# Stacked weight tails, two more separate tiles, and moved weight splits in the last stages of a transformer block

## The chip, the core and the metric

The kernel runs on one core of a Trainium2 chip. The metric is the device time of one execution in microseconds (us). The kernel before has a median of 2336.36 us over three runs (2336.26 to 2337.21). One further execution was profiled; its own time is 2338.7 us. A measurement of this kernel can tell about 0.2% from no change.

## The reference

A pre-norm transformer block on 2048 tokens of width D = 576, all in float32. The attention has 32 query heads of 18 values, with one key head and one value head that all share. The feed-forward part (FFN) is a bilinear gate without a nonlinearity and has hidden width F = 4608.

```python
h  = x + softmax((LN(x) @ wq)_heads @ (LN(x) @ wk).T / sqrt(18)) @ (LN(x) @ wv) @ wo
g, u = LN(h) @ w_gate, LN(h) @ w_up
h2 = h + (g * u) @ w_down
```

## The kernel before

**Tiles.** The tokens are cut into four blocks of 512 (block 0 to 3), the hidden width into 36 tiles of 128 (`NF`), taken in 18 pairs (`NC`). Products that need float32 accuracy are made of three passes: an operand is cast to a rounded float32 (the high part, line 88), the rest is its low part (a subtraction on VectorE, line 89), and high*high, high*low and low*high are added up on TensorE. `split` makes both parts; the engine of its cast can be given.

**The order of the work** is written out by hand: the program issues each engine's instructions in the order in which the Python code runs, and each engine works through its own list in that order, waiting where an operand is not ready. All DMAs are issued by SyncE (SP), also in order; SP also waits there until the buffer that a load writes is free.

**Stages.** (1) Layer norm, keys, values, queries and the attention of block 0. In it `sums` (line 1402) prepares on GpSimd the weights of the last stages: `t_dram` holds the tails of the gate and up weights (rows 512 to 575 of the 576, as high and low parts, two halves of 32 rows each, and their four sums), `s_dram` the sums of the other rows for the joint tiles. (2) `ffn(0)`, `ffn(1)` and `ffn(2)` go through the hidden tiles of one block each, with the attention of the later blocks put between their matmuls while pairs of it are left (`more`). `ffn(2)` stops at tile `F1` = 28; the attention ends in its tile 23, so its tiles 24 to 27 run without it. There each tile is 54 half-height matmuls of 512 columns into `gu` (line 992), and after every second tile one down product. Beside them run the last output projections of the attention for block 3 (`project`, line 754), its layer norm statistics and, by `prepare` and `transposed` (line 1057), the normalised and transposed operands of block 3 (`xh`, `bt`, `btt`). The weights of a tile are loaded to `wr` and split by `split_w`, its cast on GpSimd; GpSimd also casts `wos`, the output weights, in `split_wo`. (3) `two_blocks` (line 1240). Its first loop, here called the **separate stage**, makes tiles 0 to 27 of block 3. A tile is four products (`product`, line 1206): two into bank `jx` for the gate, two into `jy` for up. A product is seven matmuls: six on the two 128-row chunks of one weight operand, and a last one on its 96 tail rows (high, high and low part, 32 rows each). After every odd tile follows the down product of an earlier pair. The second loop, here the **joint stage**, makes tiles 28 to 35 of blocks 2 and 3 together: four weight parts against four data parts in seven products rather than eight, then again one down product per tile, for the pairs of block 2 and 3 in turn. (4) The down products of the last pair, and the output.

**The down product** (`down`, line 893) has 14 stages of three matmuls over three PSUM banks (`STAGES`). Eight stages are added to `h` by VectorE (line 954), six are copied by ScalarE (line 958) and added by GpSimd (line 959). A stage that reuses a bank waits until the bank was read.

**What feeds a product.** `ahead(tails, splits)` (line 1192) keeps two counts. Up to `tails` products it loads the tails from `t_dram` to a slot of `ws_j` (in the joint stage also of `X`), with three DMAs of 32 rows (line 1197). Up to `splits` products it casts the raw operand (ScalarE, line 88), subtracts (VectorE, line 89) and starts the load of the raw operand eight further on (line 1190). A slot is used again six products on, in the joint stage eight. `refill(n)` calls it after every product with n + 6 tails and n + 4 splits, in the joint stage n + 8 and n + 5. After a down product `finish` loads seven weight tiles `wdo` for a later one (`load_wd`, line 865). `left_parts` (line 1218) makes the left operands of the next down product in four steps, here called the left parts, and `differences` (line 1098) makes the data parts of the joint stage in some 28 steps, both as generators that the tile loop advances.

Of the kernel before, what the change touches and what calls it, by code (L numbers as in the profile page):

```python
# [25 lines left out]
P = 128  # L26
# [28 lines left out]
class Block:  # L55
# [652 lines left out]
    def split_wo(self):  # L708

        if self.wo_r and not self.wos and self.wo_round + 1 < self.round:  # L710
            c = min(self.wo_r)
            w = self.wos[c] = self.wp.tile([P, 2, D], F32R, tag="wos", bufs=1, name=f"wos{self.round}_{c}")
            self.split(w[:, 0], w[:, 1], self.wo_r.pop(c), self.nc.gpsimd.tensor_copy)
            if c == 3:
                self.load_wo(4)
# [131 lines left out]
    def load_w(self, n):  # L847

        if n < N_OLD:
            r = self.wr[n] = self.wp.tile([P, 9, P], F32, tag="wr", bufs=1, name=f"wr{n}")  # L850
            self.sp.dma_start(r, self.wgu[n % NF])

    def split_w(self, n):
        if n < N_OLD:
            r = self.wr.pop(n)
            w = self.ws[n] = self.wp.tile([P, 2, 9, P], F32R, tag="ws", bufs=2, name=f"ws{n}")
            self.split(w[:, 0], w[:, 1], r, self.nc.gpsimd.tensor_copy)
            self.load_w(n + 1)
# [333 lines left out]
    def ahead(self, tails, splits):  # L1192

        while self.n_tail < min(tails, len(SEQ)):
            f, o = SEQ[self.n_tail]
            for k in range(3):
                self.sp.dma_start(f32(self.slot(self.n_tail)[32 * k:32 * k + 32, 4]),  # L1197
                                  self.t_dram[f // 9, 32 * (k // 2):32 * (k // 2) + 32, f % 9, o])
            self.n_tail += 1
        while self.n_split < min(splits, len(SEQ)):  # L1200
            w = self.slot(self.n_split)
            self.split(w[:, 0:2], w[:, 2:4], self.raws[self.n_split % 8])
            self.load_raw_operand(self.n_split + 8)
            self.n_split += 1
# [7 lines left out]

    def refill(self, n):

        joint = n > 4 * F1
        self.ahead(n + (8 if joint else 6), n + (5 if joint else 4))

# [22 lines left out]
    def two_blocks(self, pair):  # L1240
# [10 lines left out]

        def finish(head, rest=lambda: None):
            if not head:
                rest()
                return
            b, p, parts = head
            drain(parts)
            for i, _ in enumerate(self.down(b, p)):
                if i == 3:
                    rest()  # L1260
            if not (b == 2 and p >= F1 // 2):
                self.load_wd(self.n_wd + 7)

        hid = []
        for f in range(F1):
# [3 lines left out]
            for i, (bank, B) in enumerate(((x, 0), (x, 1), (y, 0), (y, 1))):  # L1269
                self.product(bank, n, self.B[B], i % 2 == 0)  # L1270
                n += 1
                if i == 1:
                    g = self.hh.tile([P, TB], F32, tag="g", bufs=1, name=f"g3_{f}")
                    act.copy(g, x)
                self.refill(n)
                if not odd:
                    next(head[2], None)
                else:
                    next(work, None)
# [3 lines left out]
            if odd:  # L1283
                finish(head, hidden)
                queue.append((3, f // 2, self.left_parts(False, hid, A)))
                hid = []
            else:
                hidden()
                drain(head[2])
        drain(work)  # L1290
# [7 lines left out]
        for f in range(F1, NF):  # L1298
# [3 lines left out]
            for i, (bank, B, first) in enumerate(plan):  # L1302
# [12 lines left out]
                elif i == 5:  # L1315
                    add(u2, u2, z)
                    dve.tensor_tensor(h3, p1, u2, ALU.mult)
                self.refill(n)
                if head and i < 3:
                    next(head[2], None)  # L1320
# [81 lines left out]
    def sums(self):  # L1402
# [5 lines left out]
        for i in range(0, 9, 2):  # L1408
# [13 lines left out]
            for _ in range(4):  # L1422
                yield
            for k, src in enumerate((hi, r)):
                for b in range(4):
# [80 lines left out]
    def run(self):  # L1506
# [4 lines left out]
        self.s_dram = tc.dram_tile([NF - F1, P, 4, 2 * P], F32, name="s_dram")  # L1511
        self.t_dram = tc.dram_tile([4, 64, 9, 8, P], F32, name="t_dram")
        self.m_dram = tc.dram_tile([NB, 2, H, TB], F32, name="m_dram")
# [63 lines left out]
N_TMP = 5  # L1577
F1 = 28
N_OLD = 2 * NF + F1
# [133 lines left out]
```

## Time and profile before

| | us |
|---|---|
| median of three runs | 2336.36 |
| profiled execution, its own time | 2338.7 |
| span of the profile, first to last instruction | 2336.8 |
| TensorE busy | 2273.2 (97%) |
| ScalarE busy | 1462.8 (63%) |
| VectorE busy | 1266.8 (54%) |
| GpSimd busy | 778.1 (33%) |
| ffn(2) without attention, with block 3's operands (from 1816.27) | 57.87 |
| separate stage, 28 tiles in 14 pairs (from 1874.14) | 299.50 |
| joint stage, 8 tiles (from 2173.64) | 135.38 |
| end (from 2309.02) | 27.78 |

The profile's own time stands 1.9 us above its span, and 2.3 us above the median of the runs. In the rows, PE is TensorE (PEld its weight loads), ACT ScalarE, DVE VectorE, POOL GpSimd, SP SyncE, SPq the DMAs that SP issues. A timeline row gives the start, the time from the first to the last instruction of the row, engine, line, operation, output and input tiles, form and count; in brackets stands how long the engine sat idle before it, and what ended that. A row of a table by stretches gives the stretch, its length, the busy time and the number of instructions of PE, PEld, DVE, ACT and POOL, the granted TensorE clock, the DMA engines' busy share and GB/s.

### The profile page before, as it was taken

The numbers are of one execution on the slowest core, as the hardware profiler recorded it, in microseconds if no ns is written. First come the engines' busy times: TensorE is split into PE (matmuls) and PEld (weight loads), VectorE is DVE, ScalarE is ACT, GpSimd is POOL, SyncE is SP. The second block draws the span as 40 slices with busy tenths as digits, with TensorE's granted clock in tenths as the row PEclk, the third lists the DMA queues.
The fourth block names the chain that finished last, engine by engine and source line by source line (L and its number), as shares of the span: only waits on it lengthen the run. The fifth ranks groups of instructions, "written<-read, shape, count | busy, mean of one in ns | idle before, by whom it ended". The sixth has DMA issues, their size and how long they took to land.

```text
span 2336.8 us, 44958 instructions
## 1 busy us (share of the span) xinstructions
PE 2273.2 (97%) x16918; PEld 1611.0 (69%) x16918; DVE 1266.8 (54%) x2325; ACT 1462.8 (63%) x2022; POOL 778.1 (33%) x923
## 2 busy tenths in 40 slices
PE   7999999999999999999999999999999899899998
PEld 5433346777777777777777777677777687777787
DVE  8343435566657564545444464444444776555575
ACT  5899887666666656766666666666666344333343
POOL 4334104555556552323232223222222212212122
PEclk9999999999999999999999999999999999999999
DMA  5457404434443445433333434433343444555442
GB/s 171 126 169 231 145 29 140 145 140 148 143 147 136 147 137 192 138 123 120 113 124 104 131 116 137 167 120 123 123 128 115 137 134 149 168 171 161 154 121 95
DMA packets 173756, 322.18 MB, mean 138 GB/s; under 512 B 28145, under 2 KB 70001, under 8 KB 171865
## 3 DMA queue, kind: packets, MB, share of 16 engines
q1 hardware_dynamic: 173529, 319.21, 42.5%
q8 instruction: 136, 2.23, 0.4%
q14 instruction: 91, 0.75, 0.1%
HBM read 237.27 MB, written 69.30 MB: 131 GB/s over the span
## 4 chain that ended last, share of the span: by engine, by line
PE 88%; DMA 5%; DVE 4%; ACT 1%; issue 1%; SPq 1%; POOL 0%; DVEq 0%; ACTq 0%; POOLq 0%
PE pg L992 20%; PE acc L601 19%; PE y L951 17%; PE s L596 12%; PE pu L992 5%; PE jx L1211 4%; PE jy L1211 4%; PE yo L754 3%; DMA ws_j<-t_dram 2%; PE psq L448 2%; PE y L909 1%; DMA wdo<-wd_dram 1%; PE gu L992 1%; SPq L1197 1%; PE jz L1211 0%
## 5 line engine op out<-in xcount | busy, mean ns | idle before, releaser
L597 ACT ACTIVATE P<-s 128x1024 f32<-128x1024 f32 x1024 | 1036.8, 1028 | 267.1 <-PE s L596 214.4
L992 PE MATMUL pu<-X,ws 64*128 64x512 f32 x2592 | 702.7, 390 | 0.7 <-DVE hf L1032 0.5
L992 PE MATMUL pg<-X,ws 64*128 64x512 f32 x2592 | 702.5, 389 | 0.0
L992 PEld LDWEIGHTS pg<-X,ws 64*128 64x128 f32 x2592 | 479.9, 186 | 66.8 <-issue 1.2
L992 PEld LDWEIGHTS pu<-X,ws 64*128 64x128 f32 x2592 | 478.2, 186 | 19.0 <-DVE h L755 1.3
L601 PE MATMUL acc<-P,V 128*32 128x512 f32 x4096 | 487.8, 598 | 0.0
L596 PE MATMUL s<-q,kT 56*128 56x512 f32 x2048 | 451.0, 416 | 3.4 <-DVE XT L89 1.8
L951 PEld LDWEIGHTS y<-wdo,room 128*128 128x128 f32 x2856 | 392.7, 190 | 52.9 <-issue 38.4
L951 PE MATMUL y<-wdo,room 128*128 128x288 f32 x2856 | 408.9, 302 | 7.6 <-DVE h L954 7.5
L958 ACT COPY tmp<-y 128x288 f32<-128x288 f32 x408 | 162.6, 399 | 375.4 <-PE y L951 347.6
L596 PEld LDWEIGHTS s<-q,kT 56*128 56x128 f32 x2048 | 212.8, 184 | 177.5 <-ACT P L597 95.4
L959 POOL TENSOR_TENSOR h<-h,tmp 128x288 f32<-128x288 f32 x204 | 159.3, 809 | 505.3 <-ACT tmp L958 504.6
L601 PEld LDWEIGHTS acc<-P,V 128*32 128x32 f32 x4096 | 109.8, 109 | 245.7 <-issue 230.0
L959 POOL TENSOR_TENSOR x<-x,tmp 128x288 f32<-128x288 f32 x204 | 158.9, 807 | 357.2 <-ACT tmp L958 356.3
L1032 DVE TENSOR_TENSOR hf<-pu,g 128x512 f32<-128x512 f32 x96 | 66.4, 691 | 347.0 <-ACT g L1028 346.9
L89 DVE TENSOR_TENSOR ws<-wr,ws 128x1152 fp32r<-128x1152 f32 x100 | 161.4, 1614 | 80.5 <-POOL ws L88 80.5
L88 POOL CAST ws<-wr 128x1152 fp32r<-128x1152 f32 x100 | 121.3, 1213 | 245.7 <-PE pu L992 159.8
L954 DVE TENSOR_TENSOR x<-x,y 128x288 f32<-128x288 f32 x272 | 117.5, 453 | 146.2 <-PE y L951 146.2
L954 DVE TENSOR_TENSOR h<-h,y 128x288 f32<-128x288 f32 x272 | 119.1, 454 | 141.9 <-PE y L951 139.0
L1211 PE MATMUL jy<-b,ws_j 128*128 128x512 f32 x372 | 100.9, 409 | 0.0
L1211 PE MATMUL jx<-b,ws_j 128*128 128x512 f32 x372 | 97.0, 396 | 0.0
L89 DVE TENSOR_TENSOR room<-S,room 128x1024 fp32r<-128x1024 f32 x68 | 87.5, 1287 | 15.5 <-ACT room L88 15.4
(279 smaller groups left out, 2380.3 us busy)
## 6 DMA issues: line engine op xcount, KB each, us to landing
wdo<-wd_dram SPq DMA_DIRECT2D x344, 288.0 KB
wr<-in_wgu_dram SPq DMA_DIRECT2D x100, 576.0 KB
wd_dram<-wdo SPq DMA_DIRECT2D x123, 288.0 KB
q<-q_dram SPq DMA_DIRECT2D x64, 216.0 KB
raw<-in_wd_dram SPq DMA_DIRECT2D x36, 288.0 KB
wr_j<-in_wj_dram SPq DMA_DIRECT2D x68, 128.0 KB
wos_j<-in_wj_dram SPq DMA_DIRECT2D x68, 128.0 KB
t_dram<-sums SPq DMA_DIRECT2D x32, 256.0 KB
```

The lines of the kernel that those rows point to most:

```text
L88: (copy or self.cast)(hi, src)
L89: self.dve.tensor_tensor(lo, src, f32(hi), ALU.subtract)
L596: self.pe.matmul(s_[:, i], self.kT[o:o + 56, t * P:(t + 1) * P], q[o:o + 56, pr], start=True, stop=True)
L597: self.act.activation(p_, s_, AF.Exp, scale=SCALE)
L601: self.pe.matmul(acc[32 * j:32 * j + 32, :], self.V[:, t, :], Ps[j // 2][:, j % 2, :], start=(t == 0), stop=(t == NT - 1), skip_group_chec ...
L754: pe.matmul(y[:, :HD], m, k, start=(i == 0), stop=(i == len(ms) - 1))
L951: pe.matmul(y[:, :HD], m[:, t * P:(t + 1) * P], k, start=(first and j == 0), stop=(j == 2), skip_group_check=True)
L954: dve.tensor_tensor(hs, hs, y[:, :HD], ALU.add)
L958: act.copy(z, y[:, :HD])
L959: pool.tensor_tensor(hs, hs, z, ALU.add)
L992: pe.matmul(ps, w[o:o + 64, wk, c], X[o:o + 64, xk, c], start=(j == 0), stop=(j == 26))
L1211: self.pe.matmul(bank, a, m, start=(first and j == 0), stop=(j == 6), skip_group_check=True)
```

## The change

Four edits.

- **Stacked tails.** `t_dram` keeps 96 rows instead of 64: the high part is stored twice, by a third group of four stores for each of five chunks. The tail of a product is then one DMA of 96 rows, not three of 32.
- **Joint from tile 30.** `F1` goes from 28 to 30. `ffn(2)` and the separate stage make two tiles more, the joint stage two fewer. The down product of pair 13 of block 2 moves from the separate stage into `ffn(2)`.
- **Splits between stages of the down product.** `refill` asks for n + 4 splits, plus `more`. In the separate stage the odd tile's last product has no refill; in the joint stage the seventh has none. Instead `finish` refills after the down stages 7 and 11, there with one split more. The left parts are spread over both tiles of a pair (before: all in the even one), and `differences` advances one step per tile (before: four per odd tile).
- **Late weights cast by ScalarE.** `weight_cast` gives GpSimd while attention is left, then ScalarE. This reaches the splits of the `ffn(2)` weights from tile 25 on, and two of `wos`.

```diff
-            self.split(w[:, 0], w[:, 1], self.wo_r.pop(c), self.nc.gpsimd.tensor_copy)
+            self.split(w[:, 0], w[:, 1], self.wo_r.pop(c), self.weight_cast())
...
+    def weight_cast(self):
+        return self.nc.gpsimd.tensor_copy if self.more(NB) else self.act.copy
...
-            for k in range(3):
-                self.sp.dma_start(f32(self.slot(self.n_tail)[32 * k:32 * k + 32, 4]),
-                                  self.t_dram[f // 9, 32 * (k // 2):32 * (k // 2) + 32, f % 9, o])
+            self.sp.dma_start(f32(self.slot(self.n_tail)[0:96, 4]), self.t_dram[f // 9, :, f % 9, o])
...
-    def refill(self, n):
+    def refill(self, n, more=0):
...
-        self.ahead(n + (8 if joint else 6), n + (5 if joint else 4))
+        self.ahead(n + (8 if joint else 6), n + 4 + more)
...
             for i, _ in enumerate(self.down(b, p)):
                 if i == 3:
                     rest()
+                elif i in (7, 11):
+                    self.refill(n, i // 8)
...
-                self.refill(n)
-                if not odd:
+                if not odd or i < 3:
+                    self.refill(n)
+                if i in ((0, 2) if odd else (1, 3)):
                     next(head[2], None)
-                else:
+                elif i == 2 - odd:
                     next(work, None)
...
-                self.refill(n)
-                if head and i < 3:
+                if i < 6:
+                    self.refill(n)
+                if head and i in (0, 1, 2, 4):
                     next(head[2], None)
...
-            for k, src in enumerate((hi, r)):
+            for k, src in enumerate((hi, hi, r)):
                 for b in range(4):
                     sp.dma_start(self.t_dram[b, 32 * k:32 * k + 32, i:i + m], f32(src[32 * b:32 * b + 32]))
...
-F1 = 28
+F1 = 30
```

What stands on SP before, in the separate stage around the end of a down product: the last `wdo` loads of a pair, then the tails (`ws_j<-t_dram`) and the raw operands (`wos_j`) of the next products.

```order
L865 DMA wdo_2_0_22152<-wd_dram 128x576
L865 DMA wdo_2_3_22154<-wd_dram 128x576
L865 DMA wdo_2_4_22156<-wd_dram 128x576
L1197 DMA ws_j_21736<-t_dram 32x128 x3
L1190 DMA wos_j<-in_wj_dram 128x256
L1197 DMA ws_j_21736<-t_dram 32x128 x3
L1190 DMA wos_j<-in_wj_dram 128x256
L1197 DMA ws_j_21549<-t_dram 32x128 x3
```

The same place on SP after the change.

```order
L868 DMA wdo_2_0_22332<-wd_dram 128x576
L868 DMA wdo_2_3_22334<-wd_dram 128x576
L868 DMA wdo_2_4_22336<-wd_dram 128x576
L1199 DMA ws_j_21955<-t_dram 96x128 x2
L1193 DMA wos_j<-in_wj_dram 128x256
L1199 DMA ws_j_21862<-t_dram 96x128
L1193 DMA wos_j<-in_wj_dram 128x256
L1199 DMA ws_j_21862<-t_dram 96x128
```

Each product has one tail load where it had three; the raw load of a pair's first product has moved ahead of the `wdo` loads, so that two tails follow each other here.

What stands on VectorE before, at the end of an odd tile of the separate stage: a step of `differences` (L1102), a low part of a weight (L89 into `ws_j`), the eight additions of the down product (L954) with the hidden tile (L1281) among them, and the next low part.

```order
L1102 TENSOR_TENSOR raw_21674<-raw_21674,b_1_21671 128x1024
L89 TENSOR_TENSOR ws_j_21549<-wr_j,ws_j_21549 128x256
L954 TENSOR_TENSOR h_16942<-h_16942,y_0_0_22079 128x288
L954 TENSOR_TENSOR h_16942<-h_16942,y_0_1_22080 128x288
L954 TENSOR_TENSOR h_16942<-h_16942,y_0_0_22079 128x288
L1281 TENSOR_TENSOR hf_3_22077<-jy,g_3_22040 128x512
L954 TENSOR_TENSOR h_16942<-h_16942,y_0_1_22080 128x288
L954 TENSOR_TENSOR h_16942<-h_16942,y_0_0_22079 128x288
L954 TENSOR_TENSOR h_16942<-h_16942,y_0_1_22080 128x288
```

The same place on VectorE after the change; L89 into `room` is the last left part, L957 and L1286 are the lines before called L954 and L1281.

```order
L89 TENSOR_TENSOR room<-hf_1_22063,room 128x512
L957 TENSOR_TENSOR h_16950<-h_16950,y_0_0_22252 128x288
L957 TENSOR_TENSOR h_16950<-h_16950,y_0_1_22253 128x288
L957 TENSOR_TENSOR h_16950<-h_16950,y_0_0_22252 128x288
L1286 TENSOR_TENSOR hf_3_22250<-jy,g_3_22223 128x512
L957 TENSOR_TENSOR h_16950<-h_16950,y_0_1_22253 128x288
L89 TENSOR_TENSOR ws_j_21862<-wr_j,ws_j_21862 128x256
L957 TENSOR_TENSOR h_16950<-h_16950,y_0_0_22252 128x288
L957 TENSOR_TENSOR h_16950<-h_16950,y_0_1_22253 128x288
L89 TENSOR_TENSOR ws_j_21862<-wos_j,ws_j_21862 128x256
```

The weight's low part and the step of `differences` no longer stand ahead of the additions; two low parts stand between them, after the fourth and after the sixth.

What stands on ScalarE before, at the end of `ffn(2)`: the hidden gate tile of tile 27 (`g`), a left part, the four normalised rows of block 3 (`xh`), and the first cast of their transposes (`bt`).

```order
L1028 COPY g_21656<-gu_21536 128x512
L88 CAST room<-hf_21658 128x512
L1070 ACTIVATE xh_0_21666<-h_16942,mvb_21585,yb_21641 128x576
L1070 ACTIVATE xh_1_21667<-h_16942,mvb_21585,yb_21641 128x576
L1070 ACTIVATE xh_2_21668<-h_16942,mvb_21585,yb_21641 128x576
L1070 ACTIVATE xh_3_21669<-h_16942,mvb_21585,yb_21641 128x576
L88 CAST b_0_21670<-bt_21692 128x512
```

The same place on ScalarE after the change, where it lies in tile 28; `ws` is the weight of tile 29, `tmp<-y` the down product of pair 13.

```order
L88 CAST room<-S 128x1024
L88 CAST ws_21663<-wr_21558 128x1152
L1073 ACTIVATE xh_0_21676<-h_16950,mvb_21580,yb_21627 128x576
L1073 ACTIVATE xh_1_21677<-h_16950,mvb_21580,yb_21627 128x576
L1073 ACTIVATE xh_2_21678<-h_16950,mvb_21580,yb_21627 128x576
L1073 ACTIVATE xh_3_21679<-h_16950,mvb_21580,yb_21627 128x576
L961 COPY tmp<-y_13_2_21738 128x288
```

The `xh` stand now behind a weight's cast and ahead of the copies of a down product, with the matmuls of tile 28 and that down product on TensorE beside them.

More of the change, by code (lines that the diff above doesn't have):

```diff
@@ L856, in split_w @@
             w = self.ws[n] = self.wp.tile([P, 2, 9, P], F32R, tag="ws", bufs=2, name=f"ws{n}")
-            self.split(w[:, 0], w[:, 1], r, self.nc.gpsimd.tensor_copy)
+            self.split(w[:, 0], w[:, 1], r, self.weight_cast())
             self.load_w(n + 1)
@@ L1250, in two_blocks, with finish @@
         work = self.differences()
-        def finish(head, rest=lambda: None):
+        def finish(head, rest):
             if not head:
                 rest()
+                self.refill(n, 1)
                 return
@@ L1288, in two_blocks @@
                 hidden()
-                drain(head[2])
         drain(work)
@@ L1511, in run @@
         self.s_dram = tc.dram_tile([NF - F1, P, 4, 2 * P], F32, name="s_dram")
-        self.t_dram = tc.dram_tile([4, 64, 9, 8, P], F32, name="t_dram")
+        self.t_dram = tc.dram_tile([4, 96, 9, 8, P], F32, name="t_dram")
         self.m_dram = tc.dram_tile([NB, 2, H, TB], F32, name="m_dram")
```

## The prediction

> **What bounds the kernel now.** First the page: busy shares, then the chain that ended last, by engine and by line.
>
> ```profile
> span 2336.8 us, 44958 instructions
> PE 2273.2 (97%) x16918; PEld 1611.0 (69%) x16918; DVE 1266.8 (54%) x2325; ACT 1462.8 (63%) x2022; POOL 778.1 (33%) x923
> ...
> PE 88%; DMA 5%; DVE 4%; ACT 1%; issue 1%; SPq 1%; POOL 0%; DVEq 0%; ACTq 0%; POOLq 0%
> PE pg L992 20%; PE acc L601 19%; PE y L951 17%; PE s L596 12%; PE pu L992 5%; PE jx L1211 4%; PE jy L1211 4%; PE yo L754 3%; DMA ws_j<-t_dram 2%; PE psq L448 2%; PE y L909 1%; DMA wdo<-wd_dram 1%; PE gu L992 1%; SPq L1197 1%; PE jz L1211 0%
> ```
>
> TensorE bounds the kernel. The largest thing on the chain that isn't TensorE is the tail load, `ws_j<-t_dram` with 2%, and SP's issue of it (L1197) with 1%. Both lie in the last 480 us, so I read the rest by stage, in the table of busy time by stretches; the borders are starts of TensorE's instructions in the timeline.
>
> ```profile
> core 0: us, PE busy (x) PEld busy (x) DVE busy (x) ACT busy (x) POOL busy (x), PEclk, DMA share, GB/s
> 1816.27:1874.14 57.87, 49.54 (x369) 41.93 (x365) 43.82 (x95) 18.54 (x36) 15.86 (x24) 0.92 0.43 138
> 1874.14:2173.64 299.50, 274.58 (x1374) 232.69 (x1373) 178.03 (x368) 118.46 (x279) 64.89 (x83) 0.97 0.51 158
> 2173.64:2309.02 135.38, 129.01 (x647) 109.60 (x645) 90.09 (x190) 56.72 (x133) 29.03 (x38) 0.99 0.41 127
> ...
> 1838.24:1844.59 6.35, 6.35 (x55) 4.99 (x54) 5.76 (x10) 2.19 (x3) 1.95 (x2) 1.00 0.03 12
> 2003.00:2016.03 13.03, 13.03 (x59) 10.57 (x58) 9.34 (x20) 6.92 (x16) 0.80 (x1) 1.00 0.66 216
> 2016.03:2021.85 5.82, 5.82 (x43) 5.72 (x42) 4.07 (x10) 2.57 (x7) 3.77 (x5) 1.00 0.26 77
> 2044.29:2058.93 14.64, 13.27 (x58) 10.49 (x57) 7.92 (x18) 5.33 (x13) 0.92 (x2) 1.00 0.64 202
> 2064.76:2082.03 17.27, 14.34 (x58) 11.27 (x57) 7.88 (x18) 5.32 (x13) 0.87 (x2) 0.93 0.56 177
> 2244.36:2255.76 11.40, 11.40 (x52) 9.25 (x50) 8.09 (x18) 5.65 (x13) 0.79 (x2) 1.00 0.74 236
> 2255.76:2262.14 6.38, 6.06 (x43) 5.75 (x42) 4.62 (x11) 2.39 (x6) 3.86 (x6) 1.00 0.30 84
> 2020.00:2040.00 20.00, 18.20 (x83) 14.95 (x81) 9.96 (x23) 6.33 (x16) 2.75 (x4) 0.91 0.54 173
> 75.00:250.00 175.00, 175.00 (x1286) 65.90 (x1286) 65.23 (x91) 159.51 (x166) 68.39 (x62) 1.00 0.63 188
> ```
>
> The first three rows are `ffn(2)` without attention, the separate and the joint stage. Then come prices without a wait: a tile of `ffn(2)` 6.35, the eight products of a pair 13.03, a down product 5.82, the seven products of a joint tile 11.40. The two rows from 2044.29 and 2064.76 are again eight products, now 14.64 and 17.27. A pair of the separate stage could take 13.03 + 5.82 = 18.85; it takes 299.50 / 14 = 21.39. So 35.6 us of that stage are lost. The waits from 1865 to 2175 say to what:
>
> ```profile
> PEld jy L1211 <- DMA ws_j<-t_dram: 25.2, 10, 6.3
> PE jy L1211 <- DMA ws_j<-t_dram: 21.1, 10, 5.9
> ...
> PE y L951 <- DVE h L954: 2.6, 4, 1.5
> PE jx L1211 <- DMA ws_j<-t_dram: 1.2, 1, 1.2
> ```
>
> TensorE waited 22.3 us for tails (the PEld row is the same time seen by its weight loads) and 2.6 for VectorE in down products. The rest is mostly a lowered clock: 0.97 over the stage. Why the tails are late shows in SP's timeline, with the chain of the same place behind it:
>
> ```profile
> 2066.98 0.37 SPq L1190 DMA_DIRECT2D wr_j<-in_wj_dram  x1
> 2067.45 1.30 SPq L1197 DMA_DIRECT2D ws_j<-t_dram  x3
> 2068.84 0.37 SPq L1190 DMA_DIRECT2D wr_j<-in_wj_dram  x1
> 2069.31 3.22 SPq L865 DMA_DIRECT2D wdo<-wd_dram  x7
> 2072.63 1.72 SPq L1197 DMA_DIRECT2D ws_j<-t_dram  x3
> ```
>
> ```profile
> 2073.76 5.13 DMA ws_j<-t_dram
> 2078.89 0.14 issue
> 2079.02 3.21 PE jy L1211 x8
> ```
>
> From one raw load to the next SP needs 1.86 us (2066.98 to 2068.84) without waiting, a product on TensorE 13.03 / 8 = 1.63. With seven `wdo` SP needs 8 x 1.86 + 3.22 = 18.1 us per pair, as good as the 18.85 of TensorE, so every wait of its own leaves it late. Here the pair's `wdo` were issued 4.55 us after its products had begun (2069.31 against 2064.76), and the tail behind them landed at 2078.89.
>
> **The change part by part.** *Stacked tails.* Two of three tail loads go. A load of 96 rows isn't in the trace; its issue lies between a third of the 1.30 and all of it, nearest to the 0.37 of a raw load of 128 rows, so I take 0.40. SP's pair becomes 8 x (0.40 + 0.37 + 2 x 0.09) + 3.22 = 10.8 us. After the down product its last raw loads, then `wdo`, end about 2.6 us into the next products, and the first tail behind them is issued by about 3.1. If it lands 5.1 us later, it is there at 8.2; the seventh product needs it at 6 x 1.63 + 1.4 = 11.2. So the waits should go, with 3 us in hand, and the bytes per pair stay. The pair from 2003.00 backs this: same loads, 216 GB/s in its products, no wait.
>
> As the waits go, the clock should return. The row 2020 to 2040 shows 0.91 and 18.20 us busy: one gap of 1.80 us was enough. The Trainium skill, "TensorE: Matmul & The Clock Gate", asks under "Why this matters for your kernels" for no idle gaps over about 3 us; by that only the gaps above 3 us would cost clock, most of the 10.7 us left of the stage's loss (35.6 - 22.3 - 2.6) would have another cause and stay, and the sum would be some 7 us higher. With that rule this trace disagrees: 18.20 busy of 20.00 is a gap of 1.80. I price pairs by whole rows, clock included.
>
> The other side of this edit: 20 more stores to `t_dram` in the first stage. From 75 to 250 us TensorE is busy for all 175.00 us, so that attention covers them, and I take nothing. Without that cover they would cost at most some 26 us: 20 issues at 1.30, the dearest group without a wait in SP's rows above.
>
> *Splits between stages, left parts, `differences`.* The queue in question is VectorE's. Before, a weight's low part and a step of `differences` stood ahead of a down product's additions; now two low parts stand behind the fourth and the sixth. Behind them wait two additions each, and TensorE for those. The stages take 5.82 / 14 = 0.42 each, and a bank is taken up again two to three stages on. An addition and a low part need about 0.45 + 0.42, against 0.83 to 1.25 of room, so I take nothing for it, and 5.82 for a down product, with the 6.38 of the joint stage's row as the bad end. The operands of those two splits were asked for a pair earlier, so ScalarE shouldn't be held there.
>
> *Separate stage:* 15 pairs x 18.85 = 282.8, and 1.7 for a start that isn't smooth: 284.5, so -15.0 against 299.50. Bounds: 282.8 without the start (-16.7), and 15 x (13.03 + 6.38) + 3 = 294.2 with every down product at the bad end and one more tail wait like that of 2064.76 (-5.3).
>
> *Joint stage:* 6 tiles x 11.40 + 5 down products x 5.82 = 97.5, and 1.5 for the tile without a down product, where VectorE must read bank `jx` first: 99.0, so -36.4 against 135.38. Bounds: 97.5 (-37.9), and 68.4 + 5 x 6.38 + 4 = 104.3 (-31.1).
>
> *`ffn(2)` without attention.* It gains two tiles and a down product, 2 x 6.35 + 5.82 = 18.5 us. What it can win back, in TensorE's timeline:
>
> ```profile
> 1844.59 1.45 PE L951 MATMUL y<-wdo,room 128*128 128x288 f32 x9
> 1848.44 4.70 PE L951 MATMUL y<-wdo,room 128*128 128x288 f32 x33 [2.39 <-DVE h L954]
> 1852.97 3.06 PE L754 MATMUL yo<-wos,room 128*128 128x288 f32 x16
> 1855.96 6.42 PE L992 MATMUL gu<-X,ws 64*128 64x512 f32 x54
> 1867.47 0.47 PE L1081 MATMUL bt<-C,xh 128*128 128x128 f32 x1 [5.09 <-ACT xh L1070]
> 1868.23 0.47 PE L1081 MATMUL bt<-C,xh 128*128 128x128 f32 x1 [0.29 <-ACT xh L1070]
> 1868.99 0.48 PE L1081 MATMUL bt<-C,xh 128*128 128x128 f32 x1 [0.28 <-ACT xh L1070]
> 1869.75 3.03 PE L1081 MATMUL bt<-C,xh 128*128 128x128 f32 x13 [0.28 <-ACT xh L1070]
> ```
>
> TensorE stood 5.1 us before the transposes `bt`, which waited for `xh`; now tile 28 and a down product stand there. The first three transposes came every 0.76 us, the others every 3.03 / 13 = 0.23: 3 x 0.53, or 1.6, less a little. A down product stopped 2.39 us for VectorE, which had low parts queued after slow GpSimd casts; with ScalarE casting I take 0.8 of it. In all 7.0 won: +11.5 us. What is late next: the raw weight of tile 29, behind which the four `xh` now queue on ScalarE, and behind those the copies of a down product. Bounds: +18.5 with nothing won, +9.4 with all of 9.1.
>
> *Sum:* +11.5 - 15.0 - 36.4 = -39.9 us. The profiled execution's 2338.7 becomes 2298.8. The median of the runs stands 2.3 us below that, so I expect 2336.36 - 39.9 = 2296.5, rounded to 2297. The end stage stays. Of the gain, TensorE's own work is none: the tiles moved cost 18.5 + 18.85 and save 2 x (11.40 + 5.82) = 34.4, 2.9 us more.
>
> **The rivals.** *Landing binds, not SP's issue.* The tails queue in the DMA engines behind the seven `wdo`; then fewer issues bring nothing. For it: 5.13 us from issue to landing. Against it: the pair from 2003.00. The separate stage would then stay at 21.39 per pair, 15 of them 320.9 (+21.4), and with +11.5 and -33 (the joint stage keeping a first wait near 3 us) the sum is 0: 2336. The Trainium skill, "DMA: Bandwidth & Descriptors", under "Issuing engines are not separate DMA queues", speaks for this: the time a sequencer takes to start a DMA "is usually small relative to the DMA itself". With that the trace disagrees here: SP's 1.86 us per product outlast the product's 1.63.
>
> *Half of it:* tails still late by about what the row from 2044.29 shows, 14.64 - 13.03 = 1.6 per pair, 15 x 1.6 = 24 us: 2321.
>
> *Slower: the splits inside the down products hold VectorE's additions.* Place: the additions after stage 7. It decides where each of the 20 down products of the two stages loses over 2.3 us, since 20 x 2.3 = 46 eats the 39.9 and 0.2%. The down product of 1844.59 lost 1852.97 - 1844.59 - 5.82 = 2.6 to low parts ahead of its additions. At that price: +52, or 2349. Against it: those were low parts of the large weights, and casts on GpSimd; these are small and come singly.
>
> **How the numbers follow.** Forecast 0.82, half of it 0.08, landing 0.05, slower 0.05. The forecast's own ends: low -16.7 - 37.9 + 9.4 = -45, or 2291; high with two of the three stages at their bad end, +18.5 - 5.3 - 36.4 = -23, or 2313. I give 2289 to 2315, two us more on each side for the other stages. Below 0.2% (4.7 us) no change can be told. Faster: 0.82 + 0.08 and a little of landing, 0.91; same 0.04; slower 0.05.
>
> **What would show it.** In the changed profile: the tail row of the waits near zero; SP's tail issues as single ones of about 0.4 us, and `wdo` issued within 3 us of the products' start; the granted clock 1.00 in the separate stage; pairs of 18.9 us; down products of 5.8 to 6.0 with two low parts in them; no `bt` wait for `xh`. It is wrong if tails still land later than 11 us into a pair, if `y` waits for `h` grow above 1 us per down product, or if `ffn(2)`'s end grows by more than 18.5 us.

## The result, and the profile after

The changed kernel takes 2294.2 us (median of four runs, 2293.74 to 2295.41) against 2336.78 us of the kernel before in the same job (2336.26 to 2338.42). The ratio is 0.9817 (95% interval 0.98 to 0.9834). The forecast was 2297 us, its range 2289 to 2315. The profiled execution's own time is 2293.74 us, its span 2291.8.

First the page of the changed kernel: busy shares, then the chain that ended last.

```profile
PE 2264.1 (99%) x16984; PEld 1603.7 (70%) x16984; DVE 1257.6 (55%) x2315; ACT 1466.2 (64%) x2021; POOL 776.3 (34%) x910
...
PE 93%; DVE 3%; ACT 1%; DMA 1%; issue 1%; SPq 0%; POOL 0%; DVEq 0%; ACTq 0%; POOLq 0%
```

DMA fell from 5% of the chain to 1%, SP's issue from 1% to nothing. The table by stretches, in the columns of the one of before: the three stages, the products and the down product of one pair, and the products of the one pair in which a tail was late.

```profile
1816.39:1883.92 67.53, 65.37 (x518) 57.95 (x515) 49.41 (x108) 28.56 (x52) 16.27 (x26) 1.00 0.51 162
1883.92:2171.17 287.25, 286.23 (x1474) 243.72 (x1471) 192.71 (x399) 127.59 (x300) 74.51 (x89) 1.00 0.57 180
2171.17:2264.78 93.61, 92.42 (x464) 78.00 (x463) 66.16 (x136) 39.79 (x94) 21.43 (x26) 1.00 0.41 129
2037.91:2050.94 13.03, 13.03 (x58) 10.56 (x57) 8.21 (x18) 4.89 (x11) 1.07 (x2) 1.00 0.74 235
2050.94:2056.93 5.99, 5.99 (x44) 5.71 (x42) 3.73 (x9) 3.01 (x8) 3.98 (x5) 1.00 0.49 140
1980.13:1993.89 13.76, 13.32 (x59) 10.49 (x57) 8.71 (x18) 5.83 (x12) 1.08 (x2) 1.00 0.71 226
```

The clock is 1.00 in all of them. By stage, with starts of TensorE's rows as borders in both profiles:

| us | before | after | difference | forecast |
|---|---|---|---|---|
| `ffn(2)` without attention | 57.87 | 67.53 | +9.7 | +11.5 |
| separate stage | 299.50 (14 pairs) | 287.25 (15 pairs) | -12.2 | -15.0 |
| joint stage | 135.38 (8 tiles) | 93.61 (6 tiles) | -41.8 | -36.4 |
| end | 27.78 | 27.02 | -0.8 | 0 |
| sum | | | -45.1 | -39.9 |

The profile of before stood 2.3 us above its median and that of after stands 0.5 below its own, so the medians differ by about 43 us and the profiles by 45. The waits of the changed kernel from 1865 to 2175 (total, times, longest):

```profile
PE y L954 <- DVE h L957: 1.4, 2, 1.2
...
PE jy L1212 <- DMA ws_j<-t_dram: 0.4, 1, 0.4
```

Of 22.3 us of waits for tails 0.4 are left. SP's timeline shows why: here around the products that start at 2037.91.

```profile
2038.79 3.23 SPq L868 DMA_DIRECT2D wdo<-wd_dram  x7
...
2045.54 4.15 SPq L1142 DMA_DIRECT2D raw<-raw  x6
...
2050.41 0.39 SPq L1193 DMA_DIRECT2D wos_j<-in_wj_dram  x1
2050.89 0.38 SPq L1199 DMA_DIRECT2D ws_j<-t_dram  x1
2051.36 0.38 SPq L1193 DMA_DIRECT2D wr_j<-in_wj_dram  x1
```

A tail of 96 rows is issued in 0.38 us (forecast 0.40), a product costs SP 0.95 us (2050.41 to 2051.36) instead of 1.86, and `wdo` starts 0.9 us into the products, not 4.55. In this pair alone SP also has six copies of `differences` (line 1142) to issue, 4.15 us; the prediction did not count them, and they matter below.

### The profile page after: what moved, and what is told of

Its sections match the earlier page's. It is cut to its first block, busy times and chain, and to the rows that moved or that the text cites. A ratio compares the mean times of both kernels' runs of the same rounds, so it can differ in the third digit from the quotient of the medians.

```text
span 2291.8 us, 44638 instructions
## 1 busy us (share of the span) xinstructions
PE 2264.1 (99%) x16984; PEld 1603.7 (70%) x16984; DVE 1257.6 (55%) x2315; ACT 1466.2 (64%) x2021; POOL 776.3 (34%) x910
## 4 chain that ended last, share of the span: by engine, by line
PE 93%; DVE 3%; ACT 1%; DMA 1%; issue 1%; SPq 0%; POOL 0%; DVEq 0%; ACTq 0%; POOLq 0%
PE pg L995 20%; PE acc L601 20%; PE y L954 17%; PE s L596 12%; PE pu L995 6%; PE jx L1212 6%; PE jy L1212 4%; PE yo L754 3%; PE psq L448 2%; PE jz L1212 1%; PE gu L995 1%; PE y L912 1%; DMA x<-in_x_dram 0%; DVE bsa L103 0%; DVE XT L89 0%
## 5 line engine op out<-in xcount | busy, mean ns | idle before, releaser
L954 PEld LDWEIGHTS y<-wdo,room 128*128 128x128 f32 x2856 | 389.0, 188 | 49.7 <-issue 38.4
L954 PE MATMUL y<-wdo,room 128*128 128x288 f32 x2856 | 407.8, 300 | 2.7 <-DVE h L957 2.2
L962 POOL TENSOR_TENSOR h<-h,tmp 128x288 f32<-128x288 f32 x204 | 166.0, 841 | 471.4 <-ACT tmp L961 471.0
L89 DVE TENSOR_TENSOR ws<-wr,ws 128x1152 fp32r<-128x1152 f32 x102 | 163.9, 1607 | 81.3 <-POOL ws L88 81.3
L957 DVE TENSOR_TENSOR x<-x,y 128x288 f32<-128x288 f32 x272 | 117.6, 453 | 146.0 <-PE y L954 146.0
L957 DVE TENSOR_TENSOR h<-h,y 128x288 f32<-128x288 f32 x272 | 116.6, 451 | 97.0 <-PE y L954 94.6
L88 POOL CAST room<-S 128x1024 fp32r<-128x1024 f32 x45 | 64.1, 1424 | 86.1 <-DVE S L890 86.1
```

The source lines that it names most:

```text
L88: (copy or self.cast)(hi, src)
L89: self.dve.tensor_tensor(lo, src, f32(hi), ALU.subtract)
L954: pe.matmul(y[:, :HD], m[:, t * P:(t + 1) * P], k, start=(first and j == 0), stop=(j == 2), skip_group_check=True)
L957: dve.tensor_tensor(hs, hs, y[:, :HD], ALU.add)
L962: pool.tensor_tensor(hs, hs, z, ALU.add)
```

## The experiments

The theory: SP's time for issuing DMAs held the separate stage. The main rival: the landing of the bytes did. Further questions were what each of the four edits is worth, and what the splits inside the down product cost. Each group of four ran beside the kernel before, whose medians were 2336.99, 2336.53 and 2336.23 us.

| kernel | median, us (lowest to highest) | ratio to before, 95% interval |
|---|---|---|
| three loads per tail | 2333.64 (2330.89 to 2338.24) | 0.9978 to 0.9997 |
| two loads | 2299.84 (2298.9 to 2300.17) | 0.9824 to 0.9857 |
| four loads | 2405.06 (2403.02 to 2407.75) | 1.0278 to 1.0313 |
| stacked tails alone | 2304.85 (2302.43 to 2305.05) | 0.9847 to 0.988 |
| joint from tile 28 | 2296.53 (2295.27 to 2297.05) | 0.9812 to 0.9845 |
| joint from tile 32 | 2299.42 (2298.74 to 2299.77) | 0.9824 to 0.9856 |
| joint from 30 alone | 2337.19 (2334.72 to 2341.34) | 0.9995 to 1.0014 |
| old order | 2299.61 (2297.51 to 2300.96) | 0.9825 to 0.9858 |
| two more issues | 2300.31 (2298.64 to 2302.97) | 0.983 to 0.986 |
| GpSimd casts | 2297.76 (2295.76 to 2299.09) | 0.982 to 0.9847 |
| late splits | 2305.38 (2304.61 to 2307.85) | 0.985 to 0.988 |
| splits at products | 2290.52 (2289.59 to 2293.19) | 0.9791 to 0.9817 |

Differences of 3 us lie near the edge of these intervals; where one is read below, the length of the stage in the trace carries it.

### How many issues

```diff
-            self.sp.dma_start(f32(self.slot(self.n_tail)[0:96, 4]), self.t_dram[f // 9, :, f % 9, o])
+            for r in (slice(0, 32), slice(32, 64), slice(64, 96)):
+                self.sp.dma_start(f32(self.slot(self.n_tail)[r, 4]), self.t_dram[f // 9, r, f % 9, o])
```

> The changed kernel, with each tail loaded by three DMAs of 32 rows instead of one of 96: the same bytes from the same place to the same place, only three times the issues. Theory (the separate stage was held by SyncE's time for issuing, about 0.46 us a DMA, not by the landing of the bytes): a pair costs SyncE about 18.1 us again instead of 10.8, against 18.9 us of TensorE's work, so the tails come late again; the separate stage, 287.3 us after, goes back by up to 15 x 2.4 = 36 us, and the whole to 2310 to 2330 us. Rival (the landing of the bytes bound, and the stacked layout made it shorter): one issue or three makes no difference, 2294 to 2297 us.

With `(slice(0, 48), slice(48, 96))`:

> The changed kernel, with each tail loaded by two DMAs of 48 rows. Theory (SyncE's issue time, with a threshold where it meets TensorE's 18.9 us a pair): 14.4 us of SyncE a pair lies below the threshold, so next to nothing is lost, 2294 to 2298 us. Rival (each issue costs in proportion, without a threshold): about half of what three loads lose, 2302 to 2312 us. Rival (landing): 2294 to 2297 us, as with three and four loads.

With 32, 32, 16 and 16 rows:

> The changed kernel, with each tail loaded by four DMAs of 32, 32, 16 and 16 rows. Theory (SyncE's issue time): 8 x (4 x 0.46 + 0.46) + 3.22 = 21.6 us of SyncE a pair against TensorE's 18.9: each of the 15 pairs loses at least 2.7 us and the lowered clock on top, 41 us or more, 2335 to 2370 us, and more than with three loads by at least 15 x 3.5 = 50 us less what three loads still had in reserve. Rival (landing): 2294 to 2298 us.

Measured: 2333.6, 2299.8 and 2405.1 us. The bytes and their places are the same in all of them, so the landing rival (2294 to 2298 for each) falls, and so does the proportional one, which had two loads at half the loss. The loss has a threshold. With four loads SP comes to stand only at `wdo` and behind it; its timeline:

```profile
2057.38 0.37 SPq L1193 DMA_DIRECT2D wr_j<-in_wj_dram  x1
2057.84 1.76 SPq L1200 DMA_DIRECT2D ws_j<-t_dram  x4
2059.70 0.37 SPq L1193 DMA_DIRECT2D wr_j<-in_wj_dram  x1
...
2062.96 4.17 SPq L868 DMA_DIRECT2D wdo<-wd_dram  x7
2067.23 5.83 SPq L1200 DMA_DIRECT2D ws_j<-t_dram  x8
```

Each row begins 0.1 us after the one before it ends, and a product costs SP 2.3 us. Only the last two rows are longer than their issues alone (3.2 and 3.6 us). So `wdo` goes out 5.1 us into TensorE's products, which started at 2057.89 (0.9 in the changed kernel), and they wait:

```profile
2073.60 0.77 PE L1213 MATMUL jy<-tails,ws_j 96*128 96x512 f32 x1 [4.38 <-DMA ws_j<-t_dram]
2074.17 2.76 PE L1213 MATMUL jy<-b,ws_j 128*128 128x512 f32 x6
```

The expectations missed in size: two loads came out 1.8 us above their range, three 3.6, four 35. I had set SP's issuing time against TensorE's 18.9 us. But SP also stands still, and three loads show where:

```profile
2014.69 3.23 SPq L868 DMA_DIRECT2D wdo<-wd_dram  x7
2018.01 4.37 SPq L1200 DMA_DIRECT2D ws_j<-t_dram  x6
2022.95 0.35 SPq L1193 DMA_DIRECT2D wos_j<-in_wj_dram  x1
2023.79 1.23 SPq L1200 DMA_DIRECT2D ws_j<-t_dram  x3
2025.12 0.37 SPq L1193 DMA_DIRECT2D wos_j<-in_wj_dram  x1
2025.59 2.75 SPq L1200 DMA_DIRECT2D ws_j<-t_dram  x3
2028.44 0.37 SPq L1193 DMA_DIRECT2D wos_j<-in_wj_dram  x1
2028.91 1.30 SPq L1200 DMA_DIRECT2D ws_j<-t_dram  x3
2030.31 0.37 SPq L1193 DMA_DIRECT2D wr_j<-in_wj_dram  x1
...
2036.85 3.49 SPq L868 DMA_DIRECT2D wdo<-wd_dram  x7
```

Without a wait three loads take 1.30 us and a product 1.87. The six loads at 2018.01 took 4.37 instead of 2.70, the three at 2025.59 took 2.75, and two gaps of 0.57 and 0.49 stand where 0.1 is usual: 4.0 us in all. SP's own waits from 2018 to 2023 say for what:

```profile
SPq L1200 <- DMA wdo<-wd_dram: 1.6, 3, 0.7
SPq L1193 <- DMA wdo<-wd_dram: 0.5, 1, 0.5
SPq L1200 <- PE jy L1213: 0.3, 1, 0.3
```

Most of it is the landing of the `wdo` that SP has just issued, and only 0.3 us a slot that TensorE still reads. In this trace SP's DMAs use eight semaphores in turn, and before each DMA SP waits until the one eight issues earlier has landed: the `wdo` issued at 2015.63 lands at 2020.36, and the tail eight issues on starts at 2020.43. With seven `wdo` on the way only one more load goes out at once; each further one waits for another `wdo`, and these land 0.7 to 1.0 us apart. (For the 1.5 us lost in the row at 2025.59 the trace names no releaser.) This is a second wait of SP beside the one for a free buffer, and over the separate stage it makes 2.4 us per pair with three loads and 2.1 with four.

So a pair takes SP 8 x 1.87 + 3.3 = 18.3 us and 4 us of standing, together the 22.16 from one `wdo` to the next, more than TensorE's 18.9. With four loads 25.23 - 21.9 = 3.3 us of standing are left. Of 18.9 us SP has only about 15 for issuing; the landing of `wdo` takes much of the rest, so that it is a part of the cause, though not in the rival's form. The five kernels then line up (SP's time is 8 times its time per product, and 3.3):

| | SP per product | SP per pair | separate stage per pair |
|---|---|---|---|
| one load | 0.95 | 10.9 | 19.15 |
| two | 1.41 | 14.6 | 19.26 |
| one, and two small ones (next section) | 1.54 | 15.6 | 19.58 |
| three | 1.87 | 18.3 | 21.53 |
| four | 2.33 | 21.9 | 25.23 |

### Issues that carry nothing

```diff
             self.sp.dma_start(f32(self.slot(self.n_tail)[0:96, 4]), self.t_dram[f // 9, :, f % 9, o])
+            for d in (2 * self.n_tail, 2 * self.n_tail + 1):
+                self.sp.dma_start(self.extra[d % P:d % P + 1, 4 * (d // P):4 * (d // P) + 4], self.wgu[f][0:1, 0, 0:4])
```

> The changed kernel, its single load of a tail left as it is, and behind each such load two more DMAs of 16 bytes to memory that nothing reads (they leave nothing out and carry next to no bytes). Theory (the number of SyncE's issues binds, whatever they carry): three issues per product as with three loads of 32 rows, which took 2333.6 us, so 2328 to 2338 us. Rival (three loads are slow since a tail that lands in three pieces is complete later, in its landing and not in its issue): 2294 to 2298 us.

Measured: 2300.31 us, 2.3 us above the rival's range and far below the theory's. So a count of issues, whatever they carry, is not what binds, and neither is the turn of eight semaphores alone, which has three issues per product here too. SP's timeline of this kernel, around the only pair that lost more than 0.5 us (its products, from 2057.69, took 19.01):

```profile
2058.84 0.35 SPq L1194 DMA_DIRECT2D wr_j<-in_wj_dram  x1
2059.29 0.37 SPq L1200 DMA_DIRECT2D ws_j<-t_dram  x1
2059.72 0.56 SPq L1202 DMA_DIRECT2D extra<-in_wgu_dram  x2
2060.38 0.35 SPq L1194 DMA_DIRECT2D wr_j<-in_wj_dram  x1
...
2063.19 3.95 SPq L868 DMA_DIRECT2D wdo<-wd_dram  x7
```

By the median of the records an issue of one short row takes 0.25 us, of 32 rows 0.41, of 96 rows 0.38. Two small ones put 0.6 us on a product, not 0.92, and SP's pair comes to 15.6 us, on the edge of its 15. The pair that lost is the one behind six copies of `differences`, issued from 2050.68 in 3.73 us: 19.3 in all. With two loads the one late pair (2.01 us) starts at 2057.75, behind the same copies. This run lies too low to separate issue from landing in pieces. The landings in the traces do that. The first tail behind `wdo` lands 5.3 to 6.4 us after its issue in one piece (14 pairs of the changed kernel), the pieces of the late tails shown above 5.1 to 5.9 (three) and 3.9 to 5.7 us (four). So pieces don't land later; what is late is `wdo` and with it the tail's issue, since SP's round is too long.

### One edit alone, one edit undone

The kernel before, with the single load of a stacked tail and nothing else:

> The kernel before with one part of the change alone: tails stored stacked as 96 rows, one load per product; joint stage from tile 28, order of refills and GpSimd's casts as before. Theory (SyncE's issue time): the tails' waits and the clock that they lowered go, some 35 us of the separate stage, so 2299 to 2304 us, about nine tenths of the whole gain. Rival (landing): 2334 to 2338 us. Rival (the single load only helps together with the splits inside the down product): somewhere near the middle, 2315 to 2325 us.

The kernel before, with `F1 = 30` and nothing else:

> The kernel before with the joint stage from tile 30 and nothing else. Theory (SyncE's issue time still binds, so the added pair of the separate stage costs 21.4 us and the longer end of the stage before 9 to 12 us, against some 34.4 us less in the joint stage): 2332 to 2340 us, near no change. Rival (the border is the main cause of the gain): under 2310 us.

Measured: 2304.85 us (32.1 less than before) and 2337.19 (0.7 more). With stacked tails alone the separate stage takes 270.71 / 14 = 19.34 us per pair; the border alone leaves it at 321.57 / 15 = 21.44. So three quarters of the gain are the stacked tails' (I had expected nine tenths; the time is 0.9 us above the range), and the border brings nothing while SP binds.

The changed kernel, with one edit undone. Border:

```diff
-F1 = 30
+F1 = 28
```

> The changed kernel with the joint stage from tile 28 as before, all else changed. Theory (own work of TensorE: one pair of tiles of products less in the separate stages, 18.5 + 18.9 - 34.4 = 2.9 us less, against the waits and the half clock at the end of the stage before, which more products ahead of it cover, worth about 8 us): 2297 to 2302 us. Rival (where the border lies matters only by the own work): 2291 us. Rival (the transfers of the joint stage are still short, so that two more tiles there cost more): over 2305 us.

`F1 = 32`:

> The changed kernel with the joint stage from tile 32. Theory (only own work is left to change, 2.9 us more, and little is left to cover): 2296 to 2299 us. Rival (the border still covers waits, as from 28 to 30): 2288 to 2292 us.

Measured: 2296.53 us, 0.5 below the theory's range, and 2299.42, 0.4 above it. So 30 is the best of the three, by 2.3 us against 28. The intervals of these two overlap; the traces agree, with 450.5 us for the three stages together at 28 and 448.4 at 30. The own work costs 2.9, so the cover is worth about 5, not the 8 that I had put in. Without the two tiles TensorE stands before the transposes again, and the rows behind show a lowered clock. Timeline and stretch of the kernel with 28:

```profile
1866.10 0.47 PE L1084 MATMUL bt<-C,xh 128*128 128x128 f32 x1 [5.04 <-ACT xh L1073]
```

```profile
1866.10:1872.14 6.04, 5.18 (x24) 4.28 (x25) 2.86 (x6) 4.68 (x8) 2.42 (x8) 0.55 0.00 0
```

With 32 there is nothing left to cover: the down product of pair 13 takes 9.59 us, the next one 7.51, and two tails are late.

Casts:

```diff
-        return self.nc.gpsimd.tensor_copy if self.more(NB) else self.act.copy
+        return self.nc.gpsimd.tensor_copy
```

> The changed kernel with the late weights' high parts cast by GpSimd as before, not by ScalarE. Theory (what is left of the gain when the stacked tails, the order and the border are counted, 2.5 to 3 us, is the casts': they take GpSimd's long casts out of the additions of the stage ahead of the joint products): 2296 to 2299 us. Rival (ScalarE's casts only moved the delay, since the down product of pair 13 now waits 1.24 us for VectorE behind them): 2292 to 2294.5 us.

Measured: 2297.76 us, 3.6 more than the changed kernel. `ffn(2)` without attention takes 71.1 us (1817.34 to 1888.42) instead of 67.5, all of the 3.6; two of its down products wait for VectorE and take 9.89 and 8.40 us instead of 6.61 and 8.11.

Order of refills, left parts and differences (the chief lines of the edit):

```diff
-        self.ahead(n + (8 if joint else 6), n + 4 + more)
+        self.ahead(n + (8 if joint else 6), n + (5 if joint else 4))
...
-                elif i in (7, 11):
-                    self.refill(n, i // 8)
...
-                if i in ((0, 2) if odd else (1, 3)):
+                if not odd:
                     next(head[2], None)
-                elif i == 2 - odd:
+                else:
                     next(work, None)
```

> The changed kernel with the order of the weight splits, left parts and differences as before: no splits inside the down product. Theory (the order is worth little once the tails come in time: a down product that waits for left parts costs 0.2 to 0.5 us more, twice for each of 15 pairs; the products lose nothing): 2297 to 2303 us. Rival (the order carried the gain of the separate stage): over 2310 us. Rival (splits inside the down product cost more than they bring, since the down products take 5.99 us with them instead of 5.82): 2289 to 2293 us.

Measured: 2299.61 us, 5.4 more than the changed kernel, in the theory's range. The separate stage takes 290.10 us instead of 287.25, the joint stage 95.4 instead of 93.6. TensorE's timeline shows the wait in one of the down products, the view of waits (1885 to 2175) all of them:

```profile
1960.66 4.85 PE L954 MATMUL y<-wdo,room 128*128 128x288 f32 x33 [1.50 <-DVE h L957]
```

```profile
PE y L954 <- DVE h L957: 5.4, 6, 1.5
```

They all lie before 2002, while VectorE has four steps of `differences` per pair; once these are done, the old order's down products take 5.80 us, less than the new order's 5.99. So the edit has a good half and a costly half.

### The splits inside the down product

In VectorE's timeline of the changed kernel, the down product from 2050.94:

```profile
2054.53 0.46 DVE L957 TENSOR_TENSOR h<-h,y 128x288 f32<-128x288 f32 x1 [0.63 <-PE y L954]
2054.90 0.72 DVE L89 TENSOR_TENSOR ws_j<-wr_j,ws_j 128x256 fp32r<-128x256 f32 x1
2055.54 0.81 DVE L957 TENSOR_TENSOR h<-h,y 128x288 f32<-128x288 f32 x2
2056.93 0.42 DVE L89 TENSOR_TENSOR ws_j<-wos_j,ws_j 128x256 fp32r<-128x256 f32 x1 [0.58 <-ACT ws_j L88]
```

The low part takes 0.72 us where the same instruction takes 0.42 two rows on. GpSimd makes six additions from 2052.94 to 2058.03; the slow low part starts with 0.44 us left of one, the quick one with 0.12 us left. VectorE's additions behind the slow one come late, and the down product takes 5.99 us instead of 5.82. Two ways to take the split from there:

```diff
-                elif i in (7, 11):
-                    self.refill(n, i // 8)
+                elif i in (11, 13):
+                    self.refill(n, i // 13)
```

> The changed kernel with the two weight splits inside the down product after its stages 11 and 13 instead of 7 and 11. Theory (the down products take 5.97 to 6.02 us instead of 5.80 since VectorE's low part after stage 7, slowed to 0.72 us beside GpSimd's additions, holds an addition that a bank waits for; behind stage 11 none waits): 15 down products x 0.19 = 2.8 us less, 2290.5 to 2292 us. Rival (any split inside the down product costs the same): 2294 us. Rival (the later splits make the next product's weights late): over 2295 us.

```diff
-                elif i in (7, 11):
+                elif i in (7, 11) and n > 4 * F1:
...
-                if not odd or i < 3:
-                    self.refill(n)
+                self.refill(n)
```

> The changed kernel with all eight weight splits of a pair at the products again (none inside the down product) up to the joint tiles, while the left parts and the differences keep their new places. Theory (the order's 5.4 us come from the new places of left parts and differences, which took 1.5 us waits out of four early down products, and the splits inside the down product cost 0.19 us each): 2291 to 2293 us. Rival (the splits must leave the products, since VectorE has too much to do there with the differences): 2295 to 2300 us, with waits of y for h of 0.3 us and more in the down products.

Late splits: 2305.38 us, 11 more than the changed kernel. The down products did fall to 5.8, but each pair's products rose from 13.03 to about 14.0 with a wait for a tail (13 waits of up to 1.2 us). SP's timeline, for the products that start at 2021.41:

```profile
2017.37 0.36 SPq L1199 DMA_DIRECT2D ws_j<-t_dram  x1
2022.62 0.35 SPq L1193 DMA_DIRECT2D wr_j<-in_wj_dram  x1
...
2024.13 3.43 SPq L868 DMA_DIRECT2D wdo<-wd_dram  x7
2027.65 0.95 SPq L1199 DMA_DIRECT2D ws_j<-t_dram  x2
```

SP stood 4.9 us, until 2022.62, to load a raw operand into a buffer that VectorE's split (2021.59 to 2022.60, again slowed) still read; `wdo` came 2.7 us into the products instead of 0.9, and the tails behind it 6.2 instead of 4.2. The rival with the late weights was right on the sign, but what came late were tails behind SP's queue. So a split sets not only a weight: it also releases a DMA, and with it all that SP has queued behind.

Splits at the products: 2290.52 us, half a microsecond below the theory's range, and the separate stage 283.88 us, 3.4 less than the changed kernel's. The down products take 5.8 there, and no product waits for a tail. The gain of the new places for left parts and differences stays (no wait of 1.5 us), so the theory held. It is the fastest of all the kernels here, although its interval against before (0.9791 to 0.9817) overlaps with the changed kernel's; from the start of the last down products to TensorE's end it took 22.2 us in the profile, against 20.6. The same 22.2 stands in the traces with two loads, three loads and late splits; no run looked at why.

## Why the prediction was right, and where its steps were off

**Sum of the edits.** Stacked tails alone 32.1, order 5.4, casts 3.6, border 2.3: 43.4, against 42.6 measured at once. One was measured alone and three by undoing them, so that the sum need not come out; nothing large is missing.

**SP's issuing time as the bound: right**, and decisive (three, two and four loads). The step "18.1 us, as good as the 18.85" was too kind to SP: it can issue for about 15 of these, which is why the kernel before was late in most pairs. The prediction counted on SP's waits, but not on their main cause, the landing of `wdo`. It also put SP's 1.86 us per product against the Trainium skill's sentence on sequencers; that sentence compares one issue with its own DMA, and one issue of 32 rows takes 0.41 us in the profile of before, beside 5.13 to the landing, so that the trace does not disagree with it.

**The tails' reserve, forecast 3 us.** The wait did go, but more narrowly. In the pair at 2037.91 `wdo` ended 4.1 us into the products (forecast 2.6), and the first tail behind it was issued at 4.2 (3.1). Over 14 pairs that tail landed 5.3 to 6.4 us after its issue (5.1), which is 9.6 to 10.8 us into the products, and 11.7 in the late pair, where 11.2 is the limit. So 0.4 to 1.6 us were in hand, and one pair showed a sign that the prediction had named for being wrong.

**Separate stage, -15.0 against -12.2.** Products 13.03 as forecast; what remained at the start and for the one late tail was 0.97 + 0.73 = 1.7. The prediction had allowed 1.7 for the start alone, so that this sum fits by luck. The step that was off is "I take nothing" for the splits inside the down products: with them 13 of the 15 down products take 5.97 to 6.02, so 15 x 0.17 = 2.5 us; with the splits back at the products they take 5.8. The price was far from the 2.3 us per down product that the slower rival needed.

**Joint stage, -36.4 against -41.8**, outside the bounds given. The term "5 down products" was miscounted: with six tiles, one without a down product and one whose down product lies behind the border (in the end stage, before and after alike), four lie inside. 68.4 + 4 x 5.82 + 1.5 = 93.2; measured 93.6. The error hid since it was on the safe side: the two errors of these stages, 2.8 and 5.4 us, have opposite signs.

**`ffn(2)` without attention, +11.5 against +9.7.** The 5.1 us before the transposes went, as forecast. The transposes themselves (`bt` and `btt`) brought 4.0 instead of 1.6: I took 0.23 us each for their normal time, but that row, 1869.75 to 1872.57 before, stood at a granted clock of 0.50. In the changed kernel's timeline the 16 of `bt` take 1876.75 - 1874.91 = 1.84, or 0.115 each:

```profile
1869.62 1.06 PE L954 MATMUL y<-wdo,room 128*128 128x288 f32 x6 [1.24 <-DVE h L957]
1871.11 3.96 PE L954 MATMUL y<-wdo,room 128*128 128x288 f32 x27 [0.43 <-ACT tmp L961]
1874.91 1.91 PE L1084 MATMUL bt<-C,xh 128*128 128x128 f32 x16
1876.75 6.42 PE L995 MATMUL gu<-X,ws 64*128 64x512 f32 x54
```

The other down product won 1.8 (8.38 to 6.61), not 0.8. What was named as late next came: these rows show the new down product waiting for VectorE, then for a copy of ScalarE, 8.11 us instead of 5.82. ScalarE had the raw weight at 1866.57 and the four `xh` until 1870.77 ahead of the copy. So 18.5 - 5.1 - 4.0 - 1.8 + 2.3 = 9.9.

**The 20 more stores** cost nothing that can be seen: this stage begins at 1816.39 instead of 1816.27.

**The rivals.** Landing in the form given, where fewer issues bring nothing, and half are excluded by two and four loads together; the slower one had the right place and a price 14 times too high.

**The number.** By stage the forecast was off by +2.8, -5.4, -1.8 and -0.8 us, partly cancelling, and the profile of before lay 2.3 us above its median where that of after lies 0.5 below. That the median came within 3 us of the forecast is in part luck; the cause and the largest term are not.

## What to carry to other kernels

Add up what one queue has to issue per round, and set it against the round less the time in which that queue must stand, for buffers or for earlier loads to land: here about 15 of 18.9 us. Below that an issue cost next to nothing here, well above it its whole time (from three to four loads 3.7 us per pair, for SP as for the stage). A split, a cast or any step that frees a buffer also releases the loads queued behind it on the DMA queue, so that moving it by one or two microseconds can cost more than the wait it was to remove. Before a row's duration is taken as a price, look at the clock in which it was taken, and count rounds at the borders of a stage.

## What was not expected of the hardware

**The clock and short gaps.** Whether the six matmuls behind a late tail take 1.54 us or 2.1 to 2.8 shows if the clock was lowered. In the traces of before and of six of these kernels, of 23 gaps from 0.75 to 1.57 us none lowered it, of 15 from 1.80 to 2.81 seven did, of 20 from 2.93 to 7.26 all did. Two gaps in the kernel with three loads, in its timeline:

```profile
1938.01 0.61 PE L1213 MATMUL jy<-tails,ws_j 96*128 96x512 f32 x1 [2.12 <-DMA ws_j<-t_dram]
1938.41 2.77 PE L1213 MATMUL jy<-b,ws_j 128*128 128x512 f32 x6
...
2199.08 0.47 PE L1213 MATMUL jy<-tails,ws_j 96*128 96x512 f32 x1 [2.26 <-DMA ws_j<-t_dram]
2199.39 1.55 PE L1213 MATMUL jy<-b,ws_j 128*128 128x512 f32 x6
```

So the Trainium skill's 3 us ("TensorE: Matmul & The Clock Gate", "Why this matters for your kernels") is where a gap surely costs here; the prediction's single gap of 1.80 us was one of those in between, and its disagreement with the Trainium skill was too general. What decides in between stays open.

**A subtraction beside GpSimd.** VectorE's 128x256 low part takes 0.42 us alone. Beside GpSimd's additions of 0.81 us it takes 0.42 with 0.1 us of an addition left at its start, 0.72 with 0.4 left (changed kernel) and 1.01 with 0.7 left (late splits): each time it ends about 0.3 us after that addition. Where GpSimd's next addition meets a low part that has begun, it takes 1.02.

**An issue's time** grows little with what it carries: by the medians 0.25 us for one row of 16 bytes, 0.41 for 32 rows of 512 bytes, 0.38 for 96.
